# Query projections of two chunks in one burst, layer-norm scaling on GpSimd, and MLP weights loaded in pieces: a conditioned attention and MLP block on Trainium2

## The chip, the cores and the metric

The kernel runs on one core of one Trainium2 chip. The metric is the time of one execution on the device, in microseconds (us). Before the change the median of nine runs is 1253.07 us, between 1251.86 and 1254.06.

## What is computed

A transformer block whose layer norms are shifted, scaled and gated by a conditioning vector c. All tensors are bf16. There are 2048 tokens of width 448, 16 heads of width 256, a key and value cache of 2048 positions for each head, and an MLP of width 1792.

```
sa, ca, ga, sb, cb, gb = split(silu(c) @ w_mod)           # six vectors of 448
h = layernorm(x) * (1 + ca) + sa
q = h @ wq                                                # 16 heads of 256
p = softmax(q @ k_cache.T / 16);  o = p @ v_cache
x = x + ga * (o @ wo)
h = layernorm(x) * (1 + cb) + sb
x = x + gb * ((gelu(h @ w_gate) * (h @ w_up)) @ w_down)
```

## The kernel before, in words

**Tiles.** The tokens are four chunks of 512 (r = 0 to 3). The width of 448 is 3 x 128 + 64, so a contraction over it has three full pieces of 128 rows and one remainder of 64 rows. The normalized input of a chunk is kept turned, as hT: 128 partitions, four pieces, 512 tokens. The 64 columns of the remainder are copied beside themselves before the turn (`twin`, L248), so the upper 64 partitions of the fourth piece hold the same remainder again.

**Units.** Attention is 64 units, u = 4h + r, one for each head h and chunk r. A unit has 16 steps j, one for each 128 keys. A step issues: the scores of two steps ahead (`st_mms`, L310, two matmuls into a bank of the tag st), the exponential of the next step on ScalarE (L456), the addition of this step's E to a running sum esum on VectorE (DVE; L494, L496), and two matmuls of this step's E with the values into the two oT banks (L499). At the end of a unit, `finish_unit` (L459) casts one oT bank on DVE and the other on ScalarE, writes esum to DRAM (scr, L466) and reads it back transposed (esT, L471). In the next unit, DVE sums and inverts esT at step 7 (L475, L476), and at steps 9, 11, 13 and 15 two matmuls project 128 tokens with wo (`wo_tile`, L320), and DVE adds the result, scaled, to x_acc (L328).

**Query projections.** `q_proj` (L294) makes qT of one head and chunk: two banks, four matmuls each (the three full pieces and the fourth piece, whose upper 64 weight rows are zeroed by a memset in `load_wq`, L103), then one copy on DVE and one on ScalarE. The projection of head h + 1 and chunk r is placed at step 15 of unit (h, r), L418. Head 0 has its own projections in the first units.

**PSUM.** There are eight banks: three of the tag st (scores), two of the tag oT, and three of the tag mi, which everything else shares in turn (query and output projections, transposes, the modulation vectors). A new tile of a tag takes the bank that was used longest ago, and its first matmul waits until that bank has been read.

**Order.** Every engine runs its instructions in the order in which the program text issues them. A table `fills` holds further work for chosen places: `fill(u, j, f)` runs f in unit u after the oT matmuls of step j and ahead of an output projection of the same step. All DMAs but three go through the queue of SyncE (SP), in order: a DMA that waits holds up those behind it. E has eight buffers, the query tiles eight.

**Start.** `load_x`, `load_wm`, `load_wq`, `load_k` and `load_wo` are called at L150 to L159: x of chunk 0, the first part of w_mod, wq and keys of head 0, wo of head 0, the second part of w_mod, x of chunk 2, wq of head 1, x of chunk 3. The layer norm (class `LN`, L212) of a chunk has statistics on DVE (L220, L221), a reciprocal root on GpSimd (an addition and a power, L227, L228), the normalization of four tiles (`norm`, L235, on DVE L243; a variant on GpSimd with a prepared shift, `shift`, L230, is in the text and unused), and the twin copy. Chunks 0 and 1 are turned on TensorE (`transpose`, L267, read out by DVE and ScalarE). Chunks 2 and 3 are turned through DRAM (`turn`, L251: one write, four transposing reads on SP) and then scaled and shifted on DVE (`modulate`, L260). Chunks 1 to 3 are spread over units 0 to 2 by `add_ln` (L366) and the loop at L391.

**Gates and MLP.** The gate vector of the first branch, ga_bf, is made in unit 1 (L360), and then GpSimd scales wo of each head by it (`scale_wo`, L134). All MLP weights are loaded at one place, unit 13, step 8 (`load_mlp`, L426, placed at L442), 4.5 MB in five DMAs; GpSimd scales w_down by gb_bf in units 20 to 33 (L444). After attention, `gate_up` (L519) already keeps the remainder of w_gate in the lower and that of w_up in the upper 64 rows, and issues four 64-row matmuls (L533), alternating between the halves, ahead of twelve full ones (L540).

Of the kernel before, what the change touches and what calls it, by code (L numbers as in the profile page):

```python
# [7 lines left out]
P = 128  # L8
BF16 = mybir.dt.bfloat16
F32 = mybir.dt.float32  # L10
# [6 lines left out]
def kernel(  # L17
# [15 lines left out]
    nc = tc.nc  # L33
    S = A_x.shape[1]
    D = A_x.shape[2]
    H = A_k_cache.shape[1]
    SK = A_k_cache.shape[2]
    Dh = A_k_cache.shape[3]
    Df = B_w_gate.shape[1]
    NKS = SK // P  # L40
    assert Dh == 2 * P and D == 3 * P + 64 and S % 512 == 0 and SK % P == 0
    NC = S // 512
    DCH = 4
    DL = D - 3 * P
    NHC = Df // P
# [6 lines left out]
    res = pool("res", 1)  # L52
# [13 lines left out]
        out=id_bf[:], in_=id_bf[:], pattern=[[-1, P]], compare_op=ALU.is_equal,  # L66
        fill=0.0, base=0, channel_multiplier=1,
# [6 lines left out]
    WA = 2 * D + 64  # L74
# [16 lines left out]
    qpool = apool("qpool", 8)  # L91
# [6 lines left out]
    def mi_tile(shape, dt, name):  # L98
        return aps.tile(shape, dt, tag="mi", bufs=3, name=name)

    def load_wq(h):
        wq_t = wts.tile([P, DCH, Dh], BF16, name="wq_t")
        nc.gpsimd.memset(wq_t[DL:P, 3, :], 0.0)  # L103
        nc.sync.dma_start(
            out=wq_t[:, 0:3, :],
            in_=A_wq[0:384, h * Dh:(h + 1) * Dh].rearrange("(c p) d -> p c d", p=P),
        )
        nc.sync.dma_start(out=wq_t[:DL, 3, :], in_=A_wq[384:D, h * Dh:(h + 1) * Dh])
        return wq_t

    def load_k(h, parts=1):
        kT = kv.tile([P, 2, SK], BF16, name="kT")
        n = SK // parts
        for i in range(parts):
            for dc in range(2):
                nc.sync.dma_start_transpose(
                    out=kT[:, dc, i * n:(i + 1) * n],
                    in_=A_k_cache[0, h, i * n:(i + 1) * n, dc * P:(dc + 1) * P],
                )
        return kT  # L120
# [6 lines left out]
    def load_wo(h):  # L127
        wo_t = wts.tile([P, 2, D], BF16, name="wo_t")
        nc.sync.dma_start(
            out=wo_t[:], in_=A_wo[h * Dh:(h + 1) * Dh, :].rearrange("(c p) n -> p c n", p=P)  # L130
        )
        return wo_t

    def scale_wo(wo_t):  # L134
        for cc in range(2):
            nc.gpsimd.tensor_tensor(out=wo_t[:, cc, :], in0=wo_t[:, cc, :], in1=ga_bf[:], op=ALU.mult)  # L136

    def load_x(eng, r):
        eng.dma_start(
            out=x_bf[r], in_=x2d[r * 512:(r + 1) * 512, :].rearrange("(t p) d -> p t d", p=P)  # L140
        )

    def load_wm(a, b):
        nc.sync.dma_start(out=wm[:, 0:3, a:b], in_=w_mod[0:384, a:b].rearrange("(c p) n -> p c n", p=P))
        nc.sync.dma_start(out=wm[:DL, 3, a:b], in_=w_mod[384:D, a:b])
# [6 lines left out]
    wq, kTs, vs, wos = {}, {}, {}, {}  # L152
    wq[0] = load_wq(0)
    kTs[0] = load_k(0, parts=2)
    wos[0] = load_wo(0)
    load_wm(WA, 3 * D)
    load_x(nc.sync, 2)
    wq[1] = load_wq(1)
    load_x(nc.sync, 3)  # L159

    cps = mi_tile([P, DCH], F32, "cps")
    for ch in range(DCH):
# [38 lines left out]
    def mod_rep(g, tgt):  # L201
        mp = mi_tile([P, D], F32, "mp")
        for k in range(DCH):
            nc.tensor.matmul(
                mp[:], lhsT=scT_rep[:, k, :], rhs=wm[:, k, g * D:(g + 1) * D],
                start=(k == 0), stop=(k == DCH - 1),
            )
        nc.vector.tensor_copy(out=tgt[:], in_=mp[:])
# [85 lines left out]
    def q_proj(h, r):  # L294
        qT = qpool.tile([P, 2, 512], BF16, name="qT")
        hr = hT[("a", r)]
        for dc in range(2):
            qps = mi_tile([P, 512], F32, "qps")
            for ch in range(DCH):
                nc.tensor.matmul(  # L300
                    qps[:], lhsT=wq[h][:, ch, dc * P:(dc + 1) * P], rhs=hr[:, ch, :],
                    start=(ch == 0), stop=(ch == DCH - 1),
                )
            if dc == 0:
                nc.vector.tensor_copy(out=qT[:, dc, :], in_=qps[:])  # L305
            else:
                nc.scalar.copy(out=qT[:, dc, :], in_=qps[:])  # L307
        qTs[(h, r)] = qT

    def st_mms(u, j):  # L310
        h, r = units[u]
        st = aps.tile([P, 512], F32, tag="st", bufs=3, name="st")
        for dc in range(2):
            nc.tensor.matmul(  # L314
                st[:], lhsT=kTs[h][:, dc, j * P:(j + 1) * P], rhs=qTs[(h, r)][:, dc, :],
                start=(dc == 0), stop=(dc == 1),
            )
        return st
# [33 lines left out]
    def fill(u, j, f):  # L352
        fills.setdefault((u, j), []).append(f)
# [2 lines left out]
        for k in range(DCH):  # L356
            nc.vector.tensor_copy(out=scT_rep[:, k, :], in_=scT[:, k:k + 1].to_broadcast((P, P)))

    fill(0, 11, rep)
    fill(1, 3, lambda: mod_rep(2, ga_bf))  # L360
    fill(1, 4, lambda: scale_wo(wos[0]))
    fill(3, 0, lambda: load_wm(3 * D, 6 * D))
    fill(5, 4, lambda: mod_rep(5, gb_bf))
    fill(6, 4, lambda: mod_cols_out(mod_cols(3), sb_c, cb1p_c))

    def add_ln(key, src, c1p, s, js, jn, jt, jm=None):  # L366
        box = {}

        def stats(t):
            if t == 0:  # L370
                box["l"] = LN(key, src, c1p, s, mi_tile)
            box["l"].stats(t)

        for t in range(4):
            fill(*js[t], lambda t=t: stats(t))
        fill(*js[3], lambda: box["l"].rstd(0, 4))
        for t in range(4):
            fill(*jn[t], lambda t=t: box["l"].norm(t))
        fill(*jn[3], lambda: box["l"].twin(nc.vector))
        if jm is None:  # L380
            for p_ in range(2):
                fill(*jt[p_], lambda p_=p_: box["l"].transpose(p_))
        else:
            fill(*jt, lambda: box["l"].turn())
            for ch in range(DCH):
                fill(*jm[ch], lambda ch=ch: box["l"].modulate(ch))

    def at(u, *js):
        return [(u, j) for j in js]

    for r in range(1, NC):  # L391
        if r == 1:
            add_ln(("a", 1), x_bf[1], ca1p_c, sa_c, at(0, 0, 1, 2, 3), at(0, 5, 5, 6, 6), at(0, 8, 9))
            fill(0, 11, lambda: q_proj(0, 1))
        elif r == 2:
            add_ln(("a", 2), x_bf[2], ca1p_c, sa_c, at(0, 9, 10, 12, 13), at(0, 14, 14, 15, 15),
                   (0, 15), at(1, 10, 10, 11, 11))
            fill(1, 13, lambda: q_proj(0, 2))
        else:
            add_ln(("a", 3), x_bf[3], ca1p_c, sa_c, at(1, 0, 1, 2, 3), at(1, 4, 4, 5, 5),  # L400
                   (1, 6), at(2, 6, 7, 8, 9))
            fill(2, 13, lambda: q_proj(0, 3))
    for u, (h, r) in enumerate(units):
        if h + 1 < H:
            if r == 0:
                def ld(h=h):
                    kTs[h + 1] = load_k(h + 1)

                def ld2(h=h):
                    vs[h + 1] = load_v(h + 1)  # L410
                    wos[h + 1] = load_wo(h + 1)
                    if h + 2 < H:
                        wq[h + 2] = load_wq(h + 2)
                fill(u + 2 * (h == 0), 0, ld)
                fill(u + 1 + (h == 0), 8 * (h == 0), ld2)
            if r == 3:
                fill(u, 0, lambda h=h: scale_wo(wos[h + 1]))
            fill(u, 15, lambda h=h, r=r: q_proj(h + 1, r))  # L418
        if h == H - 1 and r in (2, 3):
            jm = at(u + 1, 4, 6, 8, 10) if r == 2 else [("mlp", ch) for ch in range(DCH)]  # L420
            add_ln(("b", r - 2), x_acc[r - 2], cb1p_c, sb_c, at(u, 1, 2, 4, 6), at(u, 7, 8, 9, 10),
                   (u, 10), jm)

    mlpw = {}

    def load_mlp():  # L426
        wgu = res.tile([P, 7, Df], BF16, name="wgu", tag="big")
        for i, w in enumerate((B_w_gate, B_w_up)):
            nc.sync.dma_start(
                out=wgu[:, 3 * i:3 * i + 3, :], in_=w[0:384, :].rearrange("(c p) n -> p c n", p=P)  # L430
            )
            nc.sync.dma_start(out=wgu[i * DL:(i + 1) * DL, 6, :], in_=w[384:D, :])
        wd = res.tile([P, NHC, D], BF16, name="wd")
        nc.sync.dma_start(out=wd[:], in_=B_w_down[:, :].rearrange("(c p) n -> p c n", p=P))
        mlpw["gu"], mlpw["d"] = wgu, wd

    def scale_wd(fc):
        nc.gpsimd.tensor_tensor(
            out=mlpw["d"][:, fc, :], in0=mlpw["d"][:, fc, :], in1=gb_bf[:], op=ALU.mult
        )  # L440

    fill(13, 8, load_mlp)  # L442
    for fc in range(NHC):
        fill(20 + fc, 4, lambda fc=fc: scale_wd(fc))  # L444

    NU = len(units)
    sts, Es = {}, {}
# [3 lines left out]
            sts[g] = st_mms(*divmod(g, NKS))  # L451

    def emit_exp(g):
        if g < NU * NKS:
            E = epool.tile([P, 512], BF16, name="E")
            nc.scalar.activation(out=E[:], in_=sts.pop(g)[:], func=ACTF.Exp, scale=inv_sqrt_dh)  # L456
            Es[g] = E
# [175 lines left out]
```

The softmax here doesn't subtract the row's maximum and nothing guards it: scores larger than these inputs give would overflow.

## Time and profile before

| what | value |
|---|---|
| median of nine runs | 1253.07 us |
| the profiled execution's own time | 1253.23 us |
| span of its instructions | 1251.5 us |
| a score matmul, st (L314) | 379 ns on record, x2016 |
| a query matmul, qps (L300) | 382 ns on record, x499 |
| an exponential on ScalarE (L456) | 598 ns, x1024 |
| an esum addition on DVE (L496) | 439 ns, x896 |
| a normalization of bf16 x on DVE (L243) | 479 ns, x16 |
| wo scaling on GpSimd (L136) | 1095 ns, x32 |
| DMA queues | 25.4% of 16 engines' span |

The profiled execution took 1253.23 us, 1.7 more than the span from its first to its last instruction. Matmuls are pipelined: a record of 379 ns includes a latency that the next matmul overlaps, so the cost of one in a row is read from the distance of the starts, not from the record. In a timeline, each line has the start in us, the length in us, the engine, the line of the kernel and the operation, the tiles written and read, and the count; in square brackets stands the idle time of the engine before it and what ended it. PE is TensorE, PEld its weight loads, ACT ScalarE, POOL GpSimd, SPq SyncE's DMA queue.

### The profile page before, as it was taken

What the parts mean: (1) busy time and instruction counts of PE and PEld (TensorE: products, weight loads), DVE (VectorE), ACT (ScalarE), POOL (GpSimd) and SP (SyncE); (2) the same over time, 40 slices, a digit from 0 to 9 for tenths busy, and PEclk for the clock granted to TensorE, in tenths of its full rate; (3) what the DMA queues carried; (4) which work ended last, traced back from release to release, by engine and by line L of the source; (5) the groups of instructions that cost most, each with busy time, mean ns of one, the idle gap of its engine ahead of it and who ended that gap; (6) DMA issues with size and microseconds to landing.
All of it is one profiled execution on the core that took longest, in us unless ns stands there. A gap on an engine that the chain in (4) does not pass through costs nothing.

```text
span 1251.5 us, 17200 instructions
## 1 busy us (share of the span) xinstructions
PE 1229.5 (98%) x5786; PEld 562.0 (45%) x5900; DVE 803.4 (64%) x1697; ACT 711.8 (57%) x1217; POOL 68.9 (6%) x87
## 2 busy tenths in 40 slices
PE   7999999999999999999999999999999999999998
PEld 3444444444444444444444444444444444444443
DVE  6866666656667666666666666666666666776543
ACT  4556666666666566666666666666666666652222
POOL 1100000000102010010000000000000000000000
PEclk9999999999999999999999999999999999999999
DMA  7444031272223040402222221404031220030110
GB/s 187 95 123 95 18 82 35 47 216 51 67 35 81 15 95 18 99 18 51 61 47 66 51 66 21 92 13 100 17 80 38 47 54 18 18 85 16 49 49 16
DMA packets 180650, 75.98 MB, mean 61 GB/s; under 512 B 149905, under 2 KB 171026, under 8 KB 180562
## 3 DMA queue, kind: packets, MB, share of 16 engines
q1 hardware_dynamic: 179504, 73.38, 24.7%
q10 hardware_dynamic: 1058, 1.51, 0.4%
q8 instruction: 46, 0.75, 0.3%
q14 instruction: 42, 0.34, 0.1%
HBM read 33.18 MB, written 13.37 MB: 37 GB/s over the span
## 4 chain that ended last, share of the span: by engine, by line
PE 91%; DVE 4%; DMA 2%; issue 1%; ACT 1%; POOL 1%; DVEq 0%; ACTq 0%
PE st L314 33%; PE oT L499 32%; PE qps L300 8%; PE wps L323 7%; PE dps L553 3%; PE g_ps L540 3%; PE u_ps L540 3%; DVE esum L496 1%; DMA scr<-esum 1%; PE g_ps L533 1%; DVE bst L220 1%; DMA esT<-scr 1%; DVE xn L243 0%; POOL rs L228 0%; DVE x_acc L328 0%
## 5 line engine op out<-in xcount | busy, mean ns | idle before, releaser
L456 ACT ACTIVATE E<-st 128x512 bf16<-128x512 f32 x1024 | 604.4, 598 | 299.9 <-PE st L314 292.3
L314 PE MATMUL st<-qT,kT 128*128 128x512 bf16 x2016 | 602.5, 379 | 4.2 <-DVE qT L305 0.4
L499 PE MATMUL oT<-E,v_h 128*128 128x512 bf16 x1990 | 596.5, 379 | 2.6 <-ACT E L456 0.7
L496 DVE TENSOR_TENSOR esum<-esum,E 128x512 bf16<-128x512 bf16 x896 | 393.7, 439 | 156.9 <-ACT E L456 129.4
L499 PEld LDWEIGHTS <-v_h 128*128 128x128 bf16 x2048 | 200.1, 98 | 244.3 <-DVE oTn L462 2.7
L314 PEld LDWEIGHTS <-kT 128*128 128x128 bf16 x2048 | 200.3, 98 | 229.4 <-issue 2.5
L328 DVE SCALAR_TENSOR_TENSOR x_acc<-wps,inv,x_acc 128x448 f32<-128x448 f32 x240 | 163.8, 682 | 158.2 <-PE wps L323 158.1
L323 PE MATMUL wps<-wo_t,oTn 128*128 128x448 bf16 x512 | 138.8, 352 | 0.5 <-DVE x_acc L328 0.2
L300 PE MATMUL qps<-hT,wq_t 128*128 128x512 bf16 x499 | 122.4, 382 | 2.3 <-DVE hT L262 1.2
L545 ACT ACTIVATE gl<-g_ps 128x512 bf16<-128x512 f32 x56 | 33.5, 597 | 89.9 <-PE g_ps L540 85.8
L136 POOL TENSOR_TENSOR wo_t<-wo_t,ga_bf 128x448 bf16<-128x448 bf16 x32 | 34.4, 1095 | 911.4 <-DMA wo_t<-in_A_wo_dram 462.0
L307 ACT CAST qT<-qps 128x512 bf16<-128x512 f32 x64 | 37.5, 587 | 79.3 <-PE qps L300 79.3
L300 PEld LDWEIGHTS <-wq_t 128*128 128x128 bf16 x512 | 50.4, 98 | 63.3 <-issue 4.3
L323 PEld LDWEIGHTS <-oTn 128*128 128x128 bf16 x512 | 50.1, 98 | 61.0 <-issue 0.8
L463 ACT CAST oTn<-oT 128x512 bf16<-128x512 f32 x64 | 37.6, 587 | 45.0 <-PE oT L499 45.0
L546 DVE TENSOR_TENSOR hhT<-gl,u_ps 128x512 bf16<-128x512 bf16 x56 | 38.4, 687 | 36.6 <-PE u_ps L540 36.6
L305 DVE CAST qT<-qps 128x512 bf16<-128x512 f32 x64 | 44.2, 690 | 23.4 <-PE qps L300 23.3
L540 PEld LDWEIGHTS <-wgu 128*128 128x128 bf16 x336 | 30.6, 98 | 44.8 <-issue 11.9
L475 DVE TENSOR_REDUCE inv<-esT 128x4 f32<-128x512 bf16 x64 | 43.5, 679 | 8.8 <-DMA esT<-scr 8.8
L540 PE MATMUL u_ps<-hT,wgu 128*128 128x512 bf16 x165 | 45.2, 379 | 0.3
L540 PE MATMUL g_ps<-hT,wgu 128*128 128x512 bf16 x160 | 43.9, 380 | 0.8 <-issue 0.8
L462 DVE CAST oTn<-oT 128x512 bf16<-128x512 f32 x64 | 44.2, 690 | 0.4 <-PE oT L499 0.3
(61 smaller groups left out, 274.5 us busy)
## 6 DMA issues: line engine op xcount, KB each, us to landing
scr<-esum SPq DMA_DIRECT2D x64, 128.0 KB, 2.0
wo_t<-in_A_wo_dram SPq DMA_DIRECT2D x16, 224.0 KB, 6.4
wq_t<-in_A_wq_dram SPq DMA_DIRECT2D x16, 192.0 KB, 4.8
xscr<-xn SPq DMA_DIRECT2D x6, 512.0 KB, 3.0
out_dram<-ob SPq DMA_DIRECT2D x16, 112.0 KB, 1.7
wd<-in_B_w_down_dram SPq DMA_DIRECT2D x1, 1568.0 KB, 17.6
x_all<-in_A_x_dram SPq DMA_DIRECT2D x3, 448.0 KB, 5.2
wgu<-in_B_w_gate_dram SPq DMA_DIRECT2D x1, 1344.0 KB, 9.2
```

What stands on the lines that cost most here:

```text
L300: nc.tensor.matmul(qps[:], lhsT=wq[h][:, ch, dc * P:(dc + 1) * P], rhs=hr[:, ch, :], start=(ch == 0), stop=(ch == DCH - 1),)
L305: nc.vector.tensor_copy(out=qT[:, dc, :], in_=qps[:])
L314: nc.tensor.matmul(st[:], lhsT=kTs[h][:, dc, j * P:(j + 1) * P], rhs=qTs[(h, r)][:, dc, :], start=(dc == 0), stop=(dc == 1),)
L323: nc.tensor.matmul(wps[:], lhsT=oTn[:, dc, t * P:(t + 1) * P], rhs=wos[h][:, dc, :], start=(dc == 0), stop=(dc == 1),)
L328: nc.vector.scalar_tensor_tensor(out=x_acc[r][:, t, :], in0=wps[:], scalar=inv[:, t:t + 1], in1=prev[:, t, :], op0=ALU.mult, op1=ALU.add,)
L456: nc.scalar.activation(out=E[:], in_=sts.pop(g)[:], func=ACTF.Exp, scale=inv_sqrt_dh)
L462: nc.vector.tensor_copy(out=oTn[:, 0, :], in_=oT[0][:])
L475: nc.vector.tensor_reduce(out=inv[:], in_=esT[:], axis=mybir.AxisListType.X, op=ALU.add)
L496: nc.vector.tensor_tensor(out=esum[:], in0=esum[:], in1=E[:], op=ALU.add)
L499: nc.tensor.matmul(oT[i][:], lhsT=vs[h][:, j, i * P:(i + 1) * P], rhs=E[:], start=(j == 0), stop=(j == NKS - 1),)
L540: nc.tensor.matmul(ps[fc, i][:], lhsT=wgu[:, 3 * i + ch, fc * P:(fc + 1) * P], rhs=hr[:, ch, :], start=False, stop=(ch == 2),)
L546: nc.vector.tensor_tensor(out=hhT[:, fc, :], in0=gl[:], in1=ps[fc, 1][:], op=ALU.mult)
```

## The change

**Queries.** For heads 1 to 15, two chunks are projected together (`q_pair`), at step 15 of the units with r = 1 and r = 3, in place of one chunk in every unit. Four banks are taken: three of the tag mi and one of the tag st. Four 64-row matmuls come first, alternating between the lower and the upper half of the rows, then twelve full ones. The remainder of wq is loaded into both halves of the rows (one DMA more for each head), and the memset is left to head 0. The exponential of the step after next is issued ahead of the burst, and not again in its old place.

**Layer norms.** Normalization and twin of chunks 1 to 3 are on GpSimd, with `shift` ahead of them, and the steps are moved. The turn of chunk 2 is at step 14 of unit 0, ahead of that unit's esum write; that of chunk 3 at step 10 of unit 1.

**Start.** x of chunk 2 is loaded ahead of wo of head 0 and the second part of w_mod; x of chunk 3 ahead of wq of head 1. The vector ga_bf is made at step 0 of unit 1, and wo of head 0 scaled at step 1.

**MLP weights.** They are loaded in four pieces: w_gate at step 5 of unit 14, w_up of unit 18, the halves of w_down of units 22 and 26. The scaling of w_down is in units 30 to 43.

```diff
 def load_wq(h):
-        nc.gpsimd.memset(wq_t[DL:P, 3, :], 0.0)
+        if h == 0:
+            nc.gpsimd.memset(wq_t[DL:P, 3, :], 0.0)
...
-        nc.sync.dma_start(out=wq_t[:DL, 3, :], in_=A_wq[384:D, h * Dh:(h + 1) * Dh])
+        for i in range(1 if h == 0 else 2):
+            nc.sync.dma_start(
+                out=wq_t[i * DL:(i + 1) * DL, 3, :], in_=A_wq[384:D, h * Dh:(h + 1) * Dh]
+            )
...
     kTs[0] = load_k(0, parts=2)
+    load_x(nc.sync, 2)
+    load_wm(WA, 3 * D)
     wos[0] = load_wo(0)
-    load_wm(WA, 3 * D)
-    load_x(nc.sync, 2)
+    load_x(nc.sync, 3)
     wq[1] = load_wq(1)
-    load_x(nc.sync, 3)
...
+    def q_pair(h, r0):
+        outs = []
+        for r in (r0, r0 + 1):
+            qTs[(h, r)] = qpool.tile([P, 2, 512], BF16, name="qT")
+            for dc in range(2):
+                if len(outs) < 3:
+                    qps = mi_tile([P, 512], F32, "qps")
+                else:
+                    qps = aps.tile([P, 512], F32, tag="st", bufs=3, name="qps")
+                outs.append((r, dc, qps))
+        for r, dc, qps in outs:
+            half = slice(dc * DL, (dc + 1) * DL)
+            nc.tensor.matmul(
+                qps[:], lhsT=wq[h][half, 3, dc * P:(dc + 1) * P], rhs=hT[("a", r)][half, 3, :],
+                start=True, stop=False,
+            )
+        for r, dc, qps in outs:
+            for ch in range(3):
+                nc.tensor.matmul(
+                    qps[:], lhsT=wq[h][:, ch, dc * P:(dc + 1) * P], rhs=hT[("a", r)][:, ch, :],
+                    start=False, stop=(ch == 2),
+                )
+            if dc == 0:
+                nc.vector.tensor_copy(out=qTs[(h, r)][:, dc, :], in_=qps[:])
+            else:
+                nc.scalar.copy(out=qTs[(h, r)][:, dc, :], in_=qps[:])
...
-    fill(0, 11, rep)
-    fill(1, 3, lambda: mod_rep(2, ga_bf))
-    fill(1, 4, lambda: scale_wo(wos[0]))
+    fill(0, 15, rep)
+    fill(1, 0, lambda: mod_rep(2, ga_bf))
+    fill(1, 1, lambda: scale_wo(wos[0]))
...
         fill(*js[3], lambda: box["l"].rstd(0, 4))
+        if on_pool:
+            fill(*js[3], lambda: box["l"].shift())
         for t in range(4):
-            fill(*jn[t], lambda t=t: box["l"].norm(t))
-        fill(*jn[3], lambda: box["l"].twin(nc.vector))
+            fill(*jn[t], lambda t=t: box["l"].norm(t, on_pool))
+        fill(*jn[3], lambda: box["l"].twin(nc.gpsimd if on_pool else nc.vector))
...
-        if r == 1:
-            add_ln(("a", 1), x_bf[1], ca1p_c, sa_c, at(0, 0, 1, 2, 3), at(0, 5, 5, 6, 6), at(0, 8, 9))
-            fill(0, 11, lambda: q_proj(0, 1))
-        elif r == 2:
-            add_ln(("a", 2), x_bf[2], ca1p_c, sa_c, at(0, 9, 10, 12, 13), at(0, 14, 14, 15, 15),
-                   (0, 15), at(1, 10, 10, 11, 11))
-            fill(1, 13, lambda: q_proj(0, 2))
-        else:
-            add_ln(("a", 3), x_bf[3], ca1p_c, sa_c, at(1, 0, 1, 2, 3), at(1, 4, 4, 5, 5),
-                   (1, 6), at(2, 6, 7, 8, 9))
-            fill(2, 13, lambda: q_proj(0, 3))
+    pn = dict(on_pool=True)
+    add_ln(("a", 1), x_bf[1], ca1p_c, sa_c, at(0, 0, 1, 2, 3), at(0, 3, 3, 3, 3), at(0, 10, 11), **pn)
+    fill(0, 13, lambda: q_proj(0, 1))
+    add_ln(("a", 2), x_bf[2], ca1p_c, sa_c, at(0, 6, 7, 8, 9), at(0, 9, 9, 9, 9),
+           (0, 14), at(1, 8, 9, 10, 11), **pn)
+    fill(1, 13, lambda: q_proj(0, 2))
+    add_ln(("a", 3), x_bf[3], ca1p_c, sa_c, at(1, 2, 3, 4, 5), at(1, 5, 5, 5, 5),
+           (1, 10), at(2, 6, 7, 8, 9), **pn)
+    fill(2, 13, lambda: q_proj(0, 3))
...
-            fill(u, 15, lambda h=h, r=r: q_proj(h + 1, r))
+            if r % 2:
+                fill(u, 15, lambda u=u, h=h, r=r: (emit_exp(16 * u + 17), q_pair(h + 1, r - 1)))
...
-    fill(13, 8, load_mlp)
+    fill(14, 5, lambda: load_gu(0))
+    fill(18, 5, lambda: load_gu(1))
+    fill(22, 5, lambda: load_wd(0, NHC // 2))
+    fill(26, 5, lambda: load_wd(NHC // 2, NHC))
     for fc in range(NHC):
-        fill(20 + fc, 4, lambda fc=fc: scale_wd(fc))
+        fill(30 + fc, 4, lambda fc=fc: scale_wd(fc))
...
     def emit_exp(g):
-        if g < NU * NKS:
+        if g < NU * NKS and g in sts:
```

More of the change, by code (lines that the diff above doesn't have):

```diff
@@ L364, with add_ln @@
     fill(6, 4, lambda: mod_cols_out(mod_cols(3), sb_c, cb1p_c))
-    def add_ln(key, src, c1p, s, js, jn, jt, jm=None):
+    def add_ln(key, src, c1p, s, js, jn, jt, jm=None, on_pool=False):
         box = {}
@@ L389, in at @@
         return [(u, j) for j in js]
-    for r in range(1, NC):
-        if r == 1:
-            add_ln(("a", 1), x_bf[1], ca1p_c, sa_c, at(0, 0, 1, 2, 3), at(0, 5, 5, 6, 6), at(0, 8, 9))
-            fill(0, 11, lambda: q_proj(0, 1))
-        elif r == 2:
-            add_ln(("a", 2), x_bf[2], ca1p_c, sa_c, at(0, 9, 10, 12, 13), at(0, 14, 14, 15, 15),
-                   (0, 15), at(1, 10, 10, 11, 11))
-            fill(1, 13, lambda: q_proj(0, 2))
-        else:
-            add_ln(("a", 3), x_bf[3], ca1p_c, sa_c, at(1, 0, 1, 2, 3), at(1, 4, 4, 5, 5),
-                   (1, 6), at(2, 6, 7, 8, 9))
-            fill(2, 13, lambda: q_proj(0, 3))
+    pn = dict(on_pool=True)
[7 more added lines that the diff above has]
+    fill(2, 13, lambda: q_proj(0, 3))
     for u, (h, r) in enumerate(units):
@@ L424, with load_gu, load_wd @@
     mlpw = {}
[L426 to L435, printed above, removed]
+    def load_gu(i):
+        if i == 0:
+            mlpw["gu"] = res.tile([P, 7, Df], BF16, name="wgu", tag="big")
+        w, wgu = (B_w_gate, B_w_up)[i], mlpw["gu"]
+        nc.sync.dma_start(
+            out=wgu[:, 3 * i:3 * i + 3, :], in_=w[0:384, :].rearrange("(c p) n -> p c n", p=P)
+        )
+        nc.sync.dma_start(out=wgu[i * DL:(i + 1) * DL, 6, :], in_=w[384:D, :])
+    def load_wd(a, b):
+        if a == 0:
+            mlpw["d"] = res.tile([P, NHC, D], BF16, name="wd")
+        nc.sync.dma_start(
+            out=mlpw["d"][:, a:b, :], in_=B_w_down[a * P:b * P, :].rearrange("(c p) n -> p c n", p=P)
+        )
     def scale_wd(fc):
```

## The prediction

> **What bounds the kernel now.** I read first the page's busy shares and the chain of work that ended last.
>
> ```profile
> PE 1229.5 (98%) x5786; PEld 562.0 (45%) x5900; DVE 803.4 (64%) x1697; ACT 711.8 (57%) x1217; POOL 68.9 (6%) x87
> PE 91%; DVE 4%; DMA 2%; issue 1%; ACT 1%; POOL 1%; DVEq 0%; ACTq 0%
> PE st L314 33%; PE oT L499 32%; PE qps L300 8%; PE wps L323 7%; PE dps L553 3%; PE g_ps L540 3%; PE u_ps L540 3%; DVE esum L496 1%; DMA scr<-esum 1%; PE g_ps L533 1%; DVE bst L220 1%; DMA esT<-scr 1%; DVE xn L243 0%; POOL rs L228 0%; DVE x_acc L328 0%
> ```
>
> TensorE is the bound. Is it stalled or full? In the trace's order of time, the query bursts (L300) of one unit and the next are 17.05 us apart over tens of units. Four matmuls of a key step take 0.863 us (two groups of 0.43), so one of 512 columns costs 0.2157. A unit is 16 x 0.863 = 13.81, plus 8 output-projection matmuls of 0.189 (0.378 a pair) = 1.51, plus 8 query matmuls = 1.73: 17.05. Full. A gain in the steady units must come from fewer matmul slots; stalls can only be had elsewhere.
>
> Where elsewhere? The distances name two places. First, bursts at 247.38 and 299.42 are 52.04 apart where 3 x 17.05 = 51.15 are due: 0.89 lost. The DVE timeline there, and SP's:
>
> ```profile
> 277.96 0.69 DVE L475 TENSOR_REDUCE inv<-esT 128x4 f32<-128x512 bf16 x1 [5.59 <-DMA esT<-scr]
> ```
>
> ```profile
> 264.31 3.12 SPq L466 DMA_DIRECT2D scr<-esum  x1
> 275.46 1.16 SPq L471 DMA_TRANSPOSE esT<-scr  x1
> ```
>
> The reader sees a small write that usually lands in 2.0 us (median) take 11.1, behind the 4.5 MB of MLP weights issued just before (wd took 17.6 us to land). Second, units 0 and 1. The TensorE timeline:
>
> ```profile
> 27.39 0.59 PE L499 MATMUL oT<-E,v_h 128*128 128x512 bf16 x2 [0.41 <-ACT E L456]
> ...
> 51.02 0.70 PE L300 MATMUL qps<-hT,wq_t 128*128 128x512 bf16 x2 [0.93 <-DVE hT L262]
> 52.00 1.56 PE L300 MATMUL qps<-hT,wq_t 128*128 128x512 bf16 x6 [0.28 <-DVE hT L262]
> ...
> 54.38 0.59 PE L314 MATMUL st<-qT,kT 128*128 128x512 bf16 x2 [0.44 <-DVE qT L305]
> ```
>
> Summing starts against slots, about 1.2 us goes in unit 0 around the transposes of chunk 1 and about 2.7 in unit 1, at the query matmuls of chunk 2.
>
> Third view, the best evidence for the new burst: the MLP already pairs 64-row remainders (L533), four halves and then twelve full matmuls, as the changed burst will.
>
> ```profile
> 1161.47 0.39 PE L533 MATMUL g_ps<-hT,wgu 64*128 64x512 bf16 x1
> 1161.47 0.39 PE L533 MATMUL u_ps<-hT,wgu 64*128 64x512 bf16 x1
> 1161.70 0.38 PE L533 MATMUL g_ps<-hT,wgu 64*128 64x512 bf16 x1
> 1161.70 0.38 PE L533 MATMUL u_ps<-hT,wgu 64*128 64x512 bf16 x1
> 1162.01 0.60 PE L540 MATMUL g_ps<-hT,wgu 128*128 128x512 bf16 x2
> ...
> 1164.70 0.39 PE L533 MATMUL g_ps<-hT,wgu 64*128 64x512 bf16 x1
> ```
>
> Halves of a pair start together; one block is 1164.70 - 1161.47 = 3.23 us.
>
> **What the Trainium skill says.** "TensorE: Matmul & The Clock Gate", Part 3, The mechanism: weight loads go ahead of running matmuls only into other row groups, and tiles in different row groups run concurrently. "TensorEngine Tiling (Array Packing)", Key Properties: changing the tiling mode drains the engine. The trace agrees with both: pairs start within 0.01 us, but a full matmul is followed by a half, and a half pair by a full one, after 0.31 to 0.32 rather than 0.216: 0.10 at each border. "GPSIMD Engine Reference", Key points: GpSimd shares its SBUF interfaces with VectorE and contends with two-port and two-input instructions. The trace agrees: the bf16 normalization on DVE takes 392 ns (median) but 1101 while GpSimd scales wo at 43.8 to 45.9, and an esum addition goes from 425 (median) to 1256 at worst.
>
> **The parts.**
>
> *Query bursts.* Heads 1 to 15: 30 pairs. Removed: 2 x 1.73 = 3.45 us; added: 3.23. Two slots are saved by concurrency (0.43) and one is given back at the two borders (0.21), so 0.22 a pair, 30 x 0.22 = 6.5 us, all on the bound. Head 0 keeps the old form. Do the four banks, the third of them late and the fourth a score bank, stall it? Clock it from the burst at 555.05. The three mi banks come from the output projections of steps 9, 11, 13; the last was read out by DVE at 553.53 to 554.2: 0.85 us ahead. The fourth bank's exponential is over, since its E feeds the last oT. The exponential of the step after next (moved ahead of the burst) stands behind the oTn cast on ACT (555.25, 0.59) and ends about 556.4; the later score tile that needs its bank is issued near 559.5. The pair's last query tile is ready at 555.05 + 3.23 + 0.17 = 558.45 (0.38 record less 0.216 is the latency), ACT copies it by 559.1, and the score tile that takes that bank is issued near 560.4. Even units have no burst to cover the oT casts any more; the last head shows that case: DVE's cast runs 1066.64 to 1067.3, TensorE wants the bank at 1067.46, and no time is lost (unit 60 fits its slots). So no stall: cost 0. If the 0.85 cover goes, every pair waits.
>
> *Loads and memsets.* 15 memsets (0.31 each) leave GpSimd; 15 DMAs of 32 KB join SP's queue in the load group, whose next user is the end of its unit: 0. The startup order (x2 ahead of wm and wo) only makes x2 earlier: issue at about 14.8 plus 5.2 to land is 20, wanted at about 22; wm and wo move back by about 0.6 us of issue, wanted 15 us later.
>
> *MLP pieces.* 0.89 us of stall goes. New: at most 1.5 MB in a piece (9.6 us to land in the trace, behind its sibling), issued at step 5, ten steps or some 10 us ahead of the next esum write. What is late next is a write of about 2 us with 3 to 4 us of slack: 0. The wd scaling moves ten units and stays off the path.
>
> *Unit 0.* Chunk 1's statistics end at 21.04, and the power at 22.77. GpSimd then does shift (two 128x4 operations: 0.5 from the 128x2 power's 0.75 as a ceiling, and 0.30, with 0.1 between, say 0.9) and four norms. GpSimd shows no one-input norm of this width: the floor is its memset's slope, 1.53 us for 1728 columns = 0.85 ns, x 448 + 0.2 = 0.58; the ceiling the two-input 128x448, 1.10. I take 0.8, since DVE's additions contend: 23.7 + 3.2 = 26.9 (26.0 to 28.1). TensorE reaches the transposes, now step 10, at 24.62 + 2 x 0.863 = 26.35: waits 0.6 (0 to 1.8); queued behind it are this unit's score and oT matmuls. DVE's esums meanwhile wait for GpSimd, so the hT read-outs and, behind them on ACT, the exponentials come later too. Against today's 1.2 lost I expect about 1.8: +0.6.
>
> *Unit 1.* Chunk 2's turn moves ahead of the unit's own esum write on SP: one write and four transposes, 3.1 + 5.0 us in the trace. GpSimd: chunk 1's tail ends at about 27.4, chunk 2's rstd 1.4, shift 0.9, norms 3.2, twin 0.4: 33.4. Then write, landing, transposes to about 41.6; only then the esum write (35.8 today), landing 43.7, esT at about 46.2. DVE, strictly in order, wants it at step 7 near 43.5: waits 2.7, and behind it stand the esums and all four modulations that the query matmuls of chunk 2 need. From its row sum at 47.98 to the last modulation at 52.27 the trace has 4.3 us: so 46.2 + 4.3 = 50.5, and about 51 with chunk 3's norms contending. TensorE, running clean, wants the fourth chunk at 48.6 + 0.65 = 49.2 and waits 1.8; another 0.6 follows where scores need qT, as today, and about 0.7 of small waits. 3.1 against 2.7: +0.4. Chunk 3's modulations are in unit 2, some 5 us after their data: 0.
>
> *Sum.* -6.5 - 0.9 + 0.6 + 0.4 = -6.4 us, from the profiled execution's 1253.23 (span 1251.5 and 1.7 around it): 1246.8. That run stands 0.16 above the median of nine, 1253.07; I predict 1246.7. Front bounds: from -1.5 (norm 0.58, DVE freed of norms, chunk 2 early) to +4 (norm 1.1 delays both chunks: turn at about 35.5, so esT near 48.3).
>
> **The rivals.**
>
> (a) *The front shortens*: -1.5 instead of +1.0, 1244.2. For: unit 1 starts a burst earlier and DVE loses 12 norms. Against: the esum locks and the turn ahead of the esum write.
>
> (b) *The front becomes the bound*: DVE held at the row sum until the query matmuls of unit 1 wait 4 to 5 us: +4 in all, 1253.07 - 7.4 + 4 = 1249.7. For: SP's order. Against: E has eight buffers, some 7 us of scores beyond the stop.
>
> (c) *No drain cost*: two whole slots, 30 x 0.43 = 13: 1240.2. Against: every MLP block.
>
> (d) *Slower: the pair waits for its third bank.* If DVE's read-out of the step-13 projection comes more than 0.85 us later than today, TensorE waits before the burst in each of 30 units. The gain is gone from 0.21 us a pair (6.4/30); at 0.4 it is 12 us: 1246.7 + 12 = 1258.7. For: four banks at once leave no spare. Against: DVE's load in a steady unit is unchanged, 10.84 of 17.05.
>
> (e) *The halves do not pair here* (the change does not do what it says): 16 slots plus the borders, +0.2 a pair, 1253.07 - 0.9 + 1.0 + 6 = 1259.2. Against: same rows, alternation and separate banks as L533.
>
> **How the numbers follow.** Forecast 54%, (a) 18, (b) 16, (c) 4, (d) 5, (e) 3. A measurement of this kernel can tell about 0.2% (2.5 us) from no change. Faster by more: forecast, (a), (c) and half of (b): 84%; within: the other half of (b), 8%; slower: (d) and (e), 8%. The range runs from (a)'s 1244.2, less 0.7 for the pieces I put at nothing, to (b)'s 1249.7 plus 0.8: 1243.5 to 1250.5, leaving out (c), (d), (e) and the tail of (b).
>
> **What would show it.** Right: bursts of 3.23 us in odd units, and a head (four units) of 68.2 - 0.44 = 67.8 us; halves starting together; no long row-sum wait near 280; chunk 2's write on SP ahead of unit 0's esum write, DVE waiting for esT in unit 1, norms on GpSimd of about 0.8. Wrong: heads of 68.2 or more, a wait for x_acc ahead of the halves, norms over 1.2 us, or unit 1 losing over 5 us.

## The result, and the profile after

The changed kernel takes 1245.81 us (median of nine runs, 1245.18 to 1247.95), the kernel before on the same chips 1252.92. The ratio is 0.9946, with a 95% interval from 0.9937 to 0.9954: 7.1 us faster. The forecast was 1246.7 with a range from 1243.5 to 1250.5. The profiled execution has a span of 1244.2 us, 7.3 less than before.

The shares and the chain on the page of the changed kernel:

```profile
PE 1221.6 (98%) x5786; PEld 550.4 (44%) x5900; DVE 796.6 (64%) x1682; ACT 715.3 (57%) x1217; POOL 77.3 (6%) x93
PE 93%; DVE 3%; issue 1%; DMA 1%; POOL 1%; ACT 0%; SPq 0%; DVEq 0%; ACTq 0%; POOLq 0%
```

TensorE is still the bound and still full; its busy time fell by 7.9 us, and GpSimd has 8 us more to do. Where it fell, the chain in order of time shows for the steady units, first before and then after, and TensorE's timeline for one burst after:

```profile
162.11 1.73 PE qps L300 x8
179.16 1.73 PE qps L300 x8
196.22 1.73 PE qps L300 x8
```

```profile
465.72 2.70 PE qps L332 x12
499.61 2.70 PE qps L332 x12
533.49 2.69 PE qps L332 x12
```

```profile
499.00 0.60 PE L326 MATMUL qps<-hT,wq_t 64*128 64x512 bf16 x4
499.54 2.76 PE L332 MATMUL qps<-hT,wq_t 128*128 128x512 bf16 x12
502.14 0.54 PE L354 MATMUL wps<-wo_t,oTn 128*128 128x448 bf16 x2
```

Two units take 33.89 us instead of 34.11. A slot is the 0.2157 us that one matmul of 512 columns takes in a row of them. The four halves (the 64-row matmuls) fill 0.54 us (starts 499.00 to 499.54), two and a half slots where the old form took four. Another half slot is lost ahead of them: the two attention matmuls before the burst begin at 498.47 and take two slots, to 498.90, and the halves begin 0.10 later. From 498.90 to 502.14 are 3.24 us, as in the MLP blocks: one slot less than the 16 of two old bursts.

The long wait near 280 us is gone too. In the kernel before, DVE stood idle for 5.59 us ahead of its sum over esT at 277.96; in the changed kernel the same sum of the same unit comes without a wait:

```profile
271.00 0.68 DVE L514 TENSOR_REDUCE inv<-esT 128x4 f32<-128x512 bf16 x1
```

The start is less simple. TensorE's timeline has these waits:

```profile
32.62 0.38 PE L345 MATMUL st<-qT,kT 128*128 128x512 bf16 x1 [0.38 <-ACT qT L311]
...
49.06 0.38 PE L304 MATMUL qps<-hT,wq_t 128*128 128x512 bf16 x1 [0.43 <-DVE hT L266]
49.72 1.24 PE L304 MATMUL qps<-hT,wq_t 128*128 128x512 bf16 x5 [0.28 <-DVE hT L266]
...
51.78 0.59 PE L345 MATMUL st<-qT,kT 128*128 128x512 bf16 x2 [0.44 <-DVE qT L309]
...
75.94 0.60 PE L538 MATMUL oT<-E,v_h 128*128 128x512 bf16 x2 [0.94 <-DVE oTn L501]
```

The waits for hT shrank; the first and the last were not there before. The accounts below set the ends of the units' last oT matmuls (before: 34.19, 56.10, 75.12, 92.17; after: 34.13, 53.50, 74.03, 90.47) against the slots between them.

| stretch | before: time less slots = lost | after: time less slots = lost |
|---|---|---|
| first scores (15.26 and 14.45) to the end of unit 0, the same slots | 18.93 in all | 19.68 in all, 0.75 more |
| unit 1 | 21.91 - 19.15 = 2.76 | 19.37 - 17.42 = 1.95 |
| unit 2 | 19.02 - 18.77 = 0.25 | 20.53 - 20.28 = 0.25 |
| unit 3 | 17.05 - 17.05 = 0 | 16.44 - 15.32 = 1.12 |

So the front (the changes in units 0 to 3) gave +0.75, -0.81 and +1.12; 0.81 more was won before the first scores; 30 pairs give -6.5; the stall near 280 us is gone (-0.9). The sum is -7.15, of 7.3 measured in the span. The last row holds the wait at 75.94, on the first oT matmul of unit 3: unit 2 has no query burst at its end any more.

### The profile page after: what moved, and what is told of

The parts are those of the page before. It is cut to its first block, busy times and chain, and to the rows that moved or that the text cites. A ratio compares the mean times of both kernels' runs of the same rounds, so it can differ in the third digit from the quotient of the medians.

```text
span 1244.2 us, 17140 instructions
## 1 busy us (share of the span) xinstructions
PE 1221.6 (98%) x5786; PEld 550.4 (44%) x5900; DVE 796.6 (64%) x1682; ACT 715.3 (57%) x1217; POOL 77.3 (6%) x93
## 4 chain that ended last, share of the span: by engine, by line
PE 93%; DVE 3%; issue 1%; DMA 1%; POOL 1%; ACT 0%; SPq 0%; DVEq 0%; ACTq 0%; POOLq 0%
PE oT L538 34%; PE st L345 34%; PE wps L354 7%; PE qps L332 6%; PE dps L592 3%; PE g_ps L579 3%; PE u_ps L579 3%; PE qps L326 1%; PE g_ps L572 1%; DVE esum L535 1%; PE qps L304 0%; DMA wm<-in_w_mod_dram 0%; DMA esT<-scr 0%; DVE bst L224 0%; DMA scr<-esum 0%
## 5 line engine op out<-in xcount | busy, mean ns | idle before, releaser
L332 PE MATMUL qps<-hT,wq_t 128*128 128x512 bf16 x348 | 81.3, 380 | 0.6 <-issue 0.3
L337 DVE CAST qT<-qps 128x512 bf16<-128x512 f32 x60 | 41.4, 691 | 36.4 <-PE qps L332 36.4
L332 PEld LDWEIGHTS <-wq_t 128*128 128x128 bf16 x360 | 32.7, 98 | 48.1 <-issue 12.7
```

What stands on the lines that cost most here:

```text
L332: nc.tensor.matmul(qps[:], lhsT=wq[h][:, ch, dc * P:(dc + 1) * P], rhs=hT[("a", r)][:, ch, :], start=False, stop=(ch == 2),)
L337: nc.vector.tensor_copy(out=qTs[(h, r)][:, dc, :], in_=qps[:])
```

## Experiments

### The three parts alone

The first takes only the burst, with the doubled remainder of wq and the moved exponential, to the kernel before. The second takes only the loads of the MLP weights and the later scaling. The third is the changed kernel with the other two undone.

```diff
e1_pair (on the kernel before)
-            fill(u, 15, lambda h=h, r=r: q_proj(h + 1, r))
+            if r % 2:
+                fill(u, 15, lambda u=u, h=h, r=r: (emit_exp(16 * u + 17), q_pair(h + 1, r - 1)))
...
e2_mlp (on the kernel before)
-    fill(13, 8, load_mlp)
+    fill(14, 5, lambda: load_gu(0))
...
e3_front (on the changed kernel)
+            fill(u, 15, lambda h=h, r=r: q_proj(h + 1, r))
...
+    fill(13, 8, load_mlp)
```

> Only the paired query bursts (with the doubled remainder of wq and the moved exponential) on the kernel before. Theory (one slot of 0.22 us saved in each of 30 pairs): 6.5 us, so about 1246.4, and in the steady part a distance of 33.9 us between bursts two units apart. Rival (the gain is mostly from the front or the MLP loads): under 4 us. If the early units lose cover for the casts of oT, up to 1 us less.

> Only the MLP weights in four pieces on the kernel before. Theory: the stall of 0.9 us around 280 us goes and nothing takes its place, 1252.0; units 13 to 15 then are 51.15 us. Rival: the pieces each delay a sum write or a key load, no gain or a loss.

> The changed kernel with single query bursts and the MLP weights at one place as before: the startup edits alone. Theory (unit 0 loses 0.75, unit 1 wins 0.8, unit 2 is covered by its query burst again, and the 0.8 won before the first scores is an accident of when TensorE's first query matmuls become fast): within 0.5 us of before, 1252.9. Rival (the 0.8 at the start belongs to the change of load order): 1252.1 and first scores at about 14.5 us instead of 15.3 in its trace. Rival of the record (the front costs 1 us): 1253.9.

Measured, against 1252.41 before: the pairs alone 1249.89, ratio 0.9979 (0.9973 to 0.9986); the MLP pieces alone 1252.04, ratio 0.9999 (0.9991 to 1.0007), so not told from no change; the front alone 1250.74, ratio 0.9985 (0.9979 to 0.9992). That is 2.5, 0.4 and 1.7 us, 4.6 in sum, where all together give 7.1. The theory missed on the first (6.5 expected) and on the third (0.5 at most expected). In the trace of the pieces alone the stall near 280 us is gone.

In the trace of the pairs alone, steady units are as expected: bursts at 503.57 and 537.46, 33.89 apart. What is missing begins at two waits in TensorE's timeline:

```profile
35.64 0.61 PE L531 MATMUL oT<-E,v_h 128*128 128x512 bf16 x2 [1.66 <-DVE oTn L494]
...
283.34 0.89 PE L531 MATMUL oT<-E,v_h 128*128 128x512 bf16 x2 [2.18 <-DVE oTn L494]
284.02 1.06 PE L345 MATMUL st<-qT,kT 128*128 128x512 bf16 x2
284.87 1.06 PE L531 MATMUL oT<-E,v_h 128*128 128x512 bf16 x2
```

Both waits stand at the first oT matmul of the unit after an even unit (one with r = 0 or 2, which has no query burst any more), and both are for DVE's cast of the old oT bank. At the end of unit 0 (34.0) DVE had been held by a normalization that waits for GpSimd's rstd (1.25). At the end of the even unit near 280 it had been held 5.33 us by the late esum write behind the MLP weights. Before the change a query burst of 1.73 us stood in each of these places, and TensorE worked through it while DVE caught up; it covered DVE's delay. From 228.44 to 300.25 the bursts show 4.0 us lost, where the kernel before lost 0.9.

Only 2.35 of these 4.0 us are the wait (from 280.56 to 283.34, less the two slots in it). After it TensorE runs at half rate: a pair of matmuls takes 0.85 us (284.02 to 284.87) where it takes 0.43 elsewhere, and the granted clock reads 0.50 from 283.5 to 286.9 and 1.00 on both sides. These 3.4 us at half rate cost the other 1.7. After the wait of 1.66 us at 35.64 the clock stays at 1.00. The runs divide by it: in 13 of the 21 runs the mean granted clock reads 0.999 and the time is 1249.82 to 1251.37; in the other eight it reads 1.000 and the time is 1247.87 to 1248.85, at the median 4.0 us below the kernel before. So the 2.5 us are a mixture of two values, about 2.0 and 4.0. Only one of the 13 has a trace, so that the others lost their time at the same place is inferred from the clock.

The front alone, in contrast, loses nothing on hT in unit 1 (its query burst for chunk 2 runs from 50.51 without a wait): with a single burst at the end of unit 0 TensorE comes to it 1.7 us later, and the data are there. In the account by units it loses 0.9 us more than before in unit 0 and 2.5 less in unit 1.

The pairs and the pieces together, without the front, were not run. The traces let it be estimated: from the first score to the end of unit 3 there are 76.9 us in the kernel before and 75.3 in the front alone, but 76.1 in the pairs alone, 76.0 in the changed kernel and 75.4 in a second trace of it (after_again, below). So in these traces the front wins 1.6 us beside single bursts, and between nothing and 0.7 beside the pairs.

### The MLP weights at one place, all else changed

```diff
-    fill(14, 5, lambda: load_gu(0))
-    fill(18, 5, lambda: load_gu(1))
-    fill(22, 5, lambda: load_wd(0, NHC // 2))
-    fill(26, 5, lambda: load_wd(NHC // 2, NHC))
+    fill(13, 8, load_mlp)
```

> The changed kernel with the MLP weights at one place as before. Theory (the late sum write now meets an even unit without a query burst to cover the cast of oT): 4 us lost around 280 us where before lost 0.9, so about 1249.8. Rival (the loads cost the same 0.9 with and without pairing): 1246.7.

Measured: 1249.48, ratio 0.9975 (0.9966 to 0.9984), 3.7 us above the changed kernel, as the theory had it. TensorE's timeline:

```profile
283.18 0.72 PE L530 MATMUL oT<-E,v_h 128*128 128x512 bf16 x2 [2.77 <-DVE oTn L493]
283.70 1.06 PE L345 MATMUL st<-qT,kT 128*128 128x512 bf16 x2
```

Here too the wait has a tail: the granted clock reads 0.50 from 283.5 to 287.0, which costs about 1.7 us. Six of the nine runs read a mean clock of 0.999, and three read 1.000 (1248.02, 1248.58 and 1249.37). So the same edit is worth at most about 1 us on the kernel before, and 3.7 beside the pairs, of which the wait for the cast is one part and the half rate behind it, in most runs, the other.

### Are the pairs what saves the slot, and what does a border cost?

The first puts all four 64-row matmuls on the lower half of the rows; the values stay the same, since both halves hold the same remainder. The second makes two blocks of a burst, one a chunk.

```diff
e4_same_rows
-            half = slice(dc * DL, (dc + 1) * DL)
+            half = slice(0, DL)
e5_two_blocks
-        for r, dc, qps in outs:
-            half = slice(dc * DL, (dc + 1) * DL)
-            ...
+        for two in (outs[:2], outs[2:]):
+            for r, dc, qps in two:
+                half = slice(dc * DL, (dc + 1) * DL)
+                ...
```

> The changed kernel with all four 64-row matmuls of a burst on the lower half of the rows; same values. Theory (the gain comes from pairs that run side by side): the four take four slots, 0.43 us more a pair, 30 pairs 13 us more: about 1258.8, slower than before. Rival (a 64-row matmul is itself cheaper, or the border cost goes when the halves do not alternate): at most 6 us more, under 1252.

> The changed kernel with the burst split in two blocks, one for each chunk: two 64-row matmuls, six full ones, twice. Same number of slots, two borders more a burst. Theory (a border between full and 64-row matmuls costs 0.10 us): 0.21 a pair, 30 pairs 6.4 us more, about 1252.2, the whole gain of pairing gone; bursts two units apart at 34.1. Rival (the missing slot is lost in the first block only, for instance on weight loads after the attention matmuls): no more than 1 us above the changed kernel.

Measured: 1258.96 on the same rows, ratio 1.0056 (1.0042 to 1.007), and 1252.26 with two blocks, ratio 0.9997 (0.9988 to 1.0005). Both theories held within 0.2 us, and the rivals fell. The chain of the first, in order of time:

```profile
230.10 0.97 PE qps L326 x4
...
264.41 0.97 PE qps L326 x4
```

Four halves take 0.97 us where the alternating ones take 0.54: two slots more, 34.31 us for two units. The chain of the second:

```profile
332.47 1.40 PE qps L333 x6
334.19 1.40 PE qps L333 x6
366.57 1.40 PE qps L333 x6
```

From 332.47 to 366.57 are 34.10 us, the time of two units before the change: two further borders eat exactly what the pairs save.

### The norms on DVE, in the new places

```diff
-    pn = dict(on_pool=True)
+    pn = dict(on_pool=False)
```

> The changed kernel with normalization and twin of chunks 1 to 3 on DVE, at the same steps. Theory (GpSimd's norms are not themselves a gain: DVE waits for rstd, then does them in 0.4 each, and no longer waits for GpSimd's use of the buffers): within 1 us of the changed kernel, 1245.5. Rival (moving the norms is what made unit 1 better): 2 us or more slower, 1248.

Measured: 1252.60, ratio 0.9999 (0.9991 to 1.0007), 6.8 us slower than the changed kernel. The theory fell. DVE's timeline and TensorE's:

```profile
29.88 1.31 DVE L247 TENSOR_SCALAR xn<-x_all,mv,rs 128x448 bf16<-128x448 bf16 x4 [1.48 <-POOL rs L232]
31.22 0.23 DVE L253 COPY xn<-xn 128x256 bf16<-128x256 bf16 x1
31.37 0.42 DVE L535 TENSOR_TENSOR esum<-esum,E 128x512 bf16<-128x512 bf16 x1
31.70 0.54 DVE L286 TENSOR_SCALAR hT<-tp,ca1p_c,sa_c 128x512 bf16<-128x512 bf16 x1
```

```profile
33.59 1.01 PE L538 MATMUL oT<-E,v_h 128*128 128x512 bf16 x2 [5.92 <-ACT E L495]
34.40 1.06 PE L345 MATMUL st<-qT,kT 128*128 128x512 bf16 x2
```

The norms are short, 0.33 each here. But DVE stands 1.48 us waiting for rstd, and behind it in its order is the read-out of chunk 1's transposes (31.70), for which TensorE had been ready since about 26; ScalarE waits for that read-out to write its own part of hT, and the exponentials wait behind that on ScalarE. On GpSimd the same wait holds nobody. The wait is not the whole price: the granted clock reads 0.50 from 30.4 to 37.2 us, so TensorE runs at half rate for 3.6 us after it starts again, about 1.8 us by an estimate; all 13 runs read a mean clock of 0.997. So at these steps, where the norms of chunk 2 stand ahead of chunk 1's transposes, the move is worth a wait on DVE and what follows from it, not the busy time that it takes off DVE. At the old steps, behind the transposes, norms on DVE were not run with both pairs and pieces.

### The order on SP, and what follows in units 0 and 2

The next run puts chunk 2's turn one step later, behind the esum write. The others, with the changed kernel once more on the same chip, load wo of the next head ahead of its values; do both; and do both with chunk 1's query matmuls one step earlier.

```diff
e7_turn_after
-           (0, 14), at(1, 8, 9, 10, 11), **pn)
+           (0, 15), at(1, 8, 9, 10, 11), **pn)
e8_wo_first
-                    vs[h + 1] = load_v(h + 1)
                     wos[h + 1] = load_wo(h + 1)
+                    vs[h + 1] = load_v(h + 1)
e11_both (e7 and e8), e12_both_q (these, and)
-    fill(0, 13, lambda: q_proj(0, 1))
+    fill(0, 12, lambda: q_proj(0, 1))
```

> The changed kernel with chunk 2's turn one step later, behind unit 0's esum write on SP. Theory (what the turn costs ahead of the esum write comes back as a later hT): DVE no longer waits for esT in unit 1 but waits for hT; the query matmuls of chunk 2 wait about as long or longer, 1246 to 1248. Rival (the order on SP was the loss of unit 1): unit 1 loses its 1.1 us of waits, 1244.8.

> The changed kernel, unchanged, on the same chip as the three that follow, so that they can be set against it: 1245.8.

> The changed kernel with wo of the next head loaded ahead of its values. Theory (in unit 2 GpSimd scales wo of head 1 just as the load lands, holds two esum additions on DVE up to 2.4 us, and the cast of oT behind them is late, 0.94 on TensorE with no query burst to cover it): wo lands about 3 us earlier, the scaling is over before the end of the unit, and 0.9 us goes: 1244.9. Rival (the additions would be late in any case): 1245.8 with the same wait for the cast near 75 us.

> The changed kernel with wo loaded first and the turn of chunk 2 behind the esum write. Theory: the turn alone gave 1.4, part of it because it also moved the end of unit 2 away from the scaling; 1244.2, no wait for the cast at the end of unit 2 and none for hT in unit 1. Rival (the gains are separate): 1243.5.

> As the last, with the query matmuls of chunk 1 one step earlier, at step 12 of unit 0, so that the scores of unit 1 need not wait for the copy of qT at step 14 (0.4 us in the trace of the changed kernel). Theory: the wait moves to the read-out of the transposes on DVE and ScalarE, which end about a step before; no gain, 1244.2. Rival: 0.4 to 0.8 faster, 1243.6.

| kernel | median us, range of five runs | ratio to before (interval) |
|---|---|---|
| e7_turn_after | 1244.39 (1243.47 to 1244.63) | 0.9934 (0.9921 to 0.9946) |
| after_again | 1245.96 (1245.56 to 1246.31) | 0.9947 (0.9935 to 0.9960) |
| e8_wo_first | 1244.97 (1244.67 to 1245.64) | 0.9940 (0.9928 to 0.9953) |
| e11_both | 1244.30 (1243.92 to 1244.59) | 0.9934 (0.9920 to 0.9947) |
| e12_both_q | 1242.52 (1242.21 to 1243.12) | 0.9920 (0.9908 to 0.9933) |

*The turn.* The rival held. SP's timelines, of the changed kernel and then of the run with the later turn:

```profile
32.06 0.39 SPq L257 DMA_DIRECT2D xscr<-xn  x1
35.00 5.04 SPq L260 DMA_TRANSPOSE hT<-xscr  x4
40.15 0.53 SPq L505 DMA_DIRECT2D scr<-esum  x1
42.31 1.14 SPq L510 DMA_TRANSPOSE esT<-scr  x1
```

```profile
34.81 0.40 SPq L505 DMA_DIRECT2D scr<-esum  x1
36.81 1.14 SPq L510 DMA_TRANSPOSE esT<-scr  x1
38.05 0.53 SPq L257 DMA_DIRECT2D xscr<-xn  x1
41.15 5.05 SPq L260 DMA_TRANSPOSE hT<-xscr  x4
```

In the first, esum waits for the turn, esT comes late, and DVE stands 1.53 us at 44.82. In the second, esT is long there, the turn ends at 46.2, and the modulations run from 45.6 to 49.2 without a wait: the 1.15 us that TensorE waited in unit 1 for hT and qT are gone. I had expected hT to be late instead; each piece of hT comes as it is wanted. The five runs of e7 (up to 1244.63) lie below all runs of the changed kernel (from 1245.18).

*wo.* GpSimd's timeline, and DVE's, in the changed kernel:

```profile
72.80 2.20 POOL L140 TENSOR_TENSOR wo_t<-wo_t,ga_bf 128x448 bf16<-128x448 bf16 x2 [23.94 <-DMA wo_t<-in_A_wo_dram]
```

```profile
72.86 2.42 DVE L535 TENSOR_TENSOR esum<-esum,E 128x512 bf16<-128x512 bf16 x2
75.21 0.68 DVE L501 CAST oTn<-oT 128x512 bf16<-128x512 f32 x1
```

Scaling starts as the load lands; two additions that take 0.95 elsewhere take 2.42; the cast behind them is late. With wo first, GpSimd scales from 68.35 to 70.6 and TensorE has no wait at the end of unit 2. The median is 1.0 below after_again's, as the theory had it, but the intervals overlap. The trace of after_again has only 0.20 of that wait, so the wait differs from run to run. In e7 the scaling came at 74.48, after the cast, by its timing alone; so both edits together gave no more than the turn (1244.30 and 1244.39).

*The query matmuls of chunk 1.* The theory fell, and the rival was too modest: 1.8 us below e11. In its trace neither the wait for qT at step 14 is left nor one of the two for E, and the way from the run of five score matmuls to the matmuls of ga_bf takes 19.11 us (15.32 to 34.43) where e11 takes 20.14 (16.21 to 36.35). That is 1.03; the rest fits a difference at the start, told in the last section, but was not settled. This kernel is 3.4 us below the changed one, with intervals that do not meet, and the fastest of the study. Nothing was tried beyond it.

## Why the prediction was right, step by step

**Query bursts: right in mechanism and size.** 3.24 us a burst, 0.22 a pair, 30 pairs; e4 and e5 show that concurrency gives two slots and the borders take one. That a burst of the same shape was already in the trace decided this. No bank was waited for, so rival (d) did not occur, and (c) and (e) are refuted.

**"So no stall: cost 0" for even units: true of the steady units, failed where DVE is late.** In the steady part the unit after an even one takes 15.33 us, all of it slots. But the last head was the wrong witness for the rest, for there DVE is on time, by 0.2 us. Where DVE is later than that, TensorE waits: 0.94 us at 75.94, and 1.66 and 2.18 in e1. The account names the cover of the odd burst (0.85) and what its loss costs, and does not do so for the cover that the even unit lost, a query burst of 1.73 us.

**MLP pieces: right about the trace, mis-sized as a part.** 0.9 was taken from a kernel with a burst in every unit. Beside the pairs the edit is worth 3.7, partly because TensorE ran at half rate after the longer wait, a cost that the prediction does not have. In the sum this came out right, since pairs at 6.5 and stall at 0.9 together assume that no other stall appears; that is true only with the pieces.

**Unit 0: right in size, in part by luck.** +0.6 expected, +0.75 found. A norm takes 0.80 (3.21 for four at 22.66), the value chosen; its floor came from 1.53 us over 1728 columns, which is 0.89 ns a column and not 0.85, but nothing hangs on it. The wait for the transposes is 0.26 on record where 0.6 was forecast. Not seen: the first scores of unit 1 are issued a step after the query matmuls moved to step 13, so they wait for the copy of qT (0.38).

**Unit 1: mechanism right, size off, with the wrong sign.** +0.4 expected, -0.8 found. DVE did wait for esT behind the turn, but 1.53 rather than 2.7: shift took 0.5 to 0.7 on GpSimd instead of 0.9, and all began about 1 us earlier (chunk 1's statistics ended at 20.04, not 21.04). The path to the fourth modulation was right in its members; e7 confirms the order on SP as the cause of the waits that were left. Why unit 1 won all the same was not taken apart. The front alone wins 1.6 us in its trace, near the 1.5 of rival (a); beside the pairs half of it or more goes again.

**Unit 2 on: failed.** 0 expected, 1.1 lost, by the even-unit step above with GpSimd's scaling as the reason.

**The sum: close, in part by luck.** Units 0 to 3 came to +1.06 where +1.0 was forecast, but only because unit 1 was 1.2 better than forecast and unit 3 1.1 worse. In the profiled execution the first scores came 0.8 earlier besides. The edits do not explain it; see the last section. Without these 0.8 us the two traces differ by 6.5, against 6.4 forecast. How much of that start is in the medians, which differ by 7.1, is not known.

## What to carry to other kernels

Work that is moved out of a place also takes away the cover that it gave. Go to every place it leaves, not only to the one it enters, and ask which engine was catching up behind it; here a saved slot exposed a stall of 2 to 3 us that another edit, worth nothing measurable alone, had to remove. Price a stall of TensorE by the distances of the starts after it, too: here 1.7 us at half rate came on top. Where an engine works in order, the wait of an instruction can cost more than its length: norms of 0.33 us each held DVE for 1.48 us and TensorE for 5.92. A pattern already in the kernel, timed by the distance of its starts, prices a new use of it to within a few hundredths of a microsecond.

## What the runs showed of the hardware

**The rate at the start.** In all these programs a run of query matmuls begins at 12.3 to 12.8 us, 0.43 us apart, and at some point the distance goes over to 0.216. In the trace before, and in e2, e3, e4, e5 and e7, the run of five score matmuls begins at 16.1 to 16.4; in the changed kernel, e1, e6, e8, e10, e12 and after_again at 15.2 to 15.6 (e11: 16.2). It does not follow the edits: e1 has the load order of before and began early, e7 that of the changed kernel and began late. About 0.8 us of a single profile's difference is of this kind. The views print a granted clock of 1.00 over this stretch, but the traces have no clock entry there: the first entry, at full rate, stands at 16.31 us in the trace before and at 13.18 in the changed kernel's, where the distance goes over. In the late group it stands at 15.0 to 16.3, in the early one at 13.2 to 14.2 (e8 has no entries). So the later scores go with a later full rate; what sets that moment was not tested.

**The rate after a stall.** In three traces the granted clock fell to 0.50 after TensorE had stood still: for 3.4 us in e1 (wait of 2.18 on record) and in e10 (2.77), and for 6.8 us in e6 (5.92), with 512-column matmuls 0.43 us apart. After the waits of 1.66 in e1 and 0.94 in the changed kernel it stayed at 1.00. Eight of the 21 runs of e1 show no such loss, so a wait of this length does not always bring it. Nothing was run to find what decides it.

**GpSimd beside DVE.** The Trainium skill ("GPSIMD Engine Reference", Key points) says that GpSimd shares its SBUF interfaces with VectorE and contends with instructions of two SBUF inputs. This case agrees: two bf16 additions of 128x512 on DVE, 0.95 us elsewhere, took 2.42 while GpSimd ran two 128x448 products.
